# A gated attention unit with a channel mixer: z of batch 0 turned by TensorE, loads of v, z and u moved in GpSimd's queue

## The chip, the cores and the metric

The kernel runs on one core of one Trainium2 chip. The time is the device time of the core in microseconds. Before the change it is 1044.64 us, the median of 6 runs (1041.26 to 1045.92).

## The reference

There are 8 batches, each of 3136 rows; u and v have 256 columns, z has 64. Two functions follow each other:

```python
scores = (1 / S) * z @ z.T
attn = maximum(scores, 0) ** 2
x = u * (attn @ v)                       # first function
h = x.T @ U @ V                          # rank 32, mixes the rows
m = x + h.T
out = m + maximum(m @ w_ch1, 0) @ w_ch2  # 256 -> 1024 -> 256
```

## The kernel before, in words

**Tiles.** The 3136 rows make 25 tiles of 128, the last (number 24, NF in the code) of 64 rows. The scores are symmetric, so for each tile j only 13 of 25 blocks are computed (`score`, L256: two matmuls of 64 rows, ACT's relu at L273, DVE's square at L275) and kept in `A[j]`. The other 12 blocks of an output tile are transposes of stored ones: `turn` (L293) has SP's queue turn `A[o]` into a `strip` by a transposing DMA, four outputs ahead of use.

**z.** A score needs z with its 64 columns on the partitions. `load_z` (L160) has GpSimd's queue load z, cast to bf16; `double_z` (L171) has DVE write each tile twice side by side; `turn_z` (L181) has SP's queue turn the result into `zT` by transposing DMAs; `extend_z` (L188) has DVE copy the first 12 tiles behind the last, so that blocks can wrap around. In batch 0 this is the start of everything.

**Outputs.** The loop at L739 takes a batch's 25 output tiles, i = 0 to 24, starting from tile 12 (o = (12 + i) mod 25). Outputs go in pairs that share two PSUM banks: i = 0 and 1, 2 and 3, up to 10 and 11, then tile 24 alone (i = 12), then 13 and 14 and so on. `attend_steps` (L381) gives an output's 25 steps of matmuls A x v (L333, half of the rows each; L367 for tile 24); between them `_spread` puts the score steps of other tiles, those of the next batch among them. `close_pair` (L342) adds the two banks (ACT L347, DVE L348) and multiplies by u (DVE L357) into `x_bf`. `load_u` (L313) has GpSimd's queue load the u of the pair after the one that opens; there are two u buffers, so it waits for L357 of the pair before.

**The mixer.** While batch b attends, the mixer of batch b - 1 runs beside it: `rank` (L416) at i = 0, `low_rank` (L463, its DVE step at L484) for seven chunks of tiles at i = 2, 3, 6, 7, 10, 11, 14, each followed by `turn_x` (L439), a transposing DMA of `x_bf` into `ut` on SP's queue. After outputs 4, 8, 13 and 17 come two bursts each (`bursts_of`, L557): the up matmuls of a chunk (L499, relu on ACT at L506) merged with the down matmuls of the chunk before (L530), each finished pair stored by GpSimd's queue (L549) once DVE has made `o_sb` (L541). The last batch's mixer stands alone at the end.

**What orders the work.** [...] All plain loads and stores stand in GpSimd's queue (POOL), all transposing DMAs in SP's. A POOL instruction that waits holds everything behind it: an out store waits for DVE's L541, a u load for L357. For the next batch, `load_z` stands at i = 1, `double_z` at 5, `turn_z` at 7 and 10, `extend_z` at 11, and the nine parts of v at i = 1, 3, 4, 5, 7, 8, 10, 11, 12 (in batch 0: z loaded in `start_up`, the rest at 9, 11, 13 and 14, and v parts at 8, 9, 10, 12, 14 to 18). Two buffers hold v, by the parity of the batch.

**The opening.** `start_up` (L575) loads z of batch 0 in three parts, then v tiles 8 to 11, doubles and turns z, and holds GpSimd's other v loads back by a copy that reads `zT` (L584). Then scores and matmuls of the first eight outputs run together, and weights and z of batch 1 are loaded.

Of the kernel before, what the change touches and what calls it, by code (L numbers as in the profile page):

```python
# [42 lines left out]
def kernel(  # L43
# [61 lines left out]
    def pair_psum():  # L105
        return ps2_pool.tile([P, 2, 512], FP32, name="ps2")
# [9 lines left out]
    zT = persist.tile([P, NT + HALF, P], BF16, name="zT")  # L116
    zT_flat = zT.rearrange("p t c -> p (t c)")
    v_both = [persist.tile([P, NT, D], BF16, name=f"v{k}") for k in range(2)]
    x_bf = persist.tile([P, XR // 4, 4 * D], BF16, name="x_bf")
    A = [persist.tile([P, NB * P], BF16, name=f"A{j}") for j in range(NT)]  # L120

# [33 lines left out]
        return ap.rearrange("p (t a c) -> p t a c", a=ND, c=P)  # L155


    z_tiles = {}

    def load_z(b, parts):  # L160
        z_c = stage.tile([P, NT, dqk], BF16, name="z_c")
        for t0, t1 in parts:
            pool_dma(out=z_c[:, t0:t1, :], in_=rows(z[b])[:, t0:t1, :])
        for r in halves:
            pool_dma(out=z_c[r, NF, :], in_=z[b, NF * P :, :])
        z_tiles[b] = z_c

    def upto(t1):
        return t1 if t1 < NF else NT

    def double_z(b, parts):  # L171
        z_c = z_tiles[b]
        z_bf = stage.tile([P, NT, 2, dqk], BF16, name="z_bf")
        z_tiles[b] = z_bf
        for t0, t1 in parts:
            for h in range(2):
                nc.vector.tensor_copy(
                    out=z_bf[:, t0 : upto(t1), h, :], in_=z_c[:, t0 : upto(t1), :]
                )

    def turn_z(b, parts):  # L181
        z_bf = z_tiles[b]
        for t0, t1 in parts:
            transpose(
                out=zT[:, t0 : upto(t1), :],
                in_=z_bf[:, t0 : upto(t1), :, :].rearrange("p t h c -> p (t h c)"),
            )
    def extend_z():  # L188
        nc.vector.tensor_copy(out=zT[:, NT:, :], in_=zT[:, :HALF, :])
# [185 lines left out]
    def after(b, o):  # L375

        t0, n = pair_of(o)
        i = place(t0) + n
        return (b, turns(i)) if i < NT else (b + 1, turns(0))

    def attend_steps(b, o):  # L381
        t0, n = pair_of(o)
        last = t0 + n - 1
        js = [(o - k) % NT if k < NB else (o + k - HALF) % NT for k in range(NT)]
        js.remove(NF)

        def step(i):
            if i == 0 and o == t0:
                open_pair(b, o)
                if after(b, o)[0] < B:  # L390
                    load_u(*after(b, o))
            if o == NF:
                if i < NT - 1 and i % 2:
                    for n in (i - 1, i):
                        for h in range(2):
                            quarter(b, js[n], n, h)
                elif i == NT - 1:
                    quarter(b, NF, i, 0)
# [12 lines left out]
        return [lambda i=i: step(i) for i in range(NT)]  # L411


# [161 lines left out]
    def start_up():  # L575
        parts = ((8, 16), (0, 8), (16, NF))
        load_z(0, parts)
        v_parts = [(8, 12), (12, 18), (3, 8), (0, 3), (18, NF), (NF, NT)]
        load_v(0, v_parts[0])
        double_z(0, parts)  # L580
        turn_z(0, parts)
        extend_z()
        mark = small.tile([P, D], BF16, name="mark", tag="t1_sb")
        nc.gpsimd.tensor_copy(out=mark[:1, :1], in_=zT[:1, 7, :1])  # L584
        for part in v_parts[1:]:
            load_v(0, part)
        nc.gpsimd.memset(U_bf[:, NF, :], 0.0)
        outs = [FIRST + i for i in range(NG)]
        c0 = FIRST * P
# [15 lines left out]
        def make(pair):  # L605
            if all(LEAD - 1 - HALF <= j < FIRST for j in pair):
                todo = []
                for j in pair:
                    at = (FIRST - j) * P
                    where[j] = A[j][:, at : at + NG * P]  # L610
                    todo.append((j, c0, NG * P, where[j]))
                score(todo)
            else:
                room = rooms.pop(0)
                for i, j in enumerate(pair):
                    where[j] = room[:, i, :]
                score([(j, c0, NG * P, room) for j in pair])
# [9 lines left out]
                seen.append(j)  # L627

        for i, pair in enumerate(pairs):
            make(pair)  # L630
            if i > 5 and i % 2:
                nxt.pop(0)()
            if i > 1:
                use(pairs[i - 2])
# [82 lines left out]
    def run(steps):  # L717
        for s in steps:
            s()
# [5 lines left out]
    for b in range(B):  # L725
        more = b + 1 < B
        begin = 0 if b else 2 * NG
        bursts = bursts_of(b - 1) if b else []
        burst_at = {4: (0, 1), 8: (2, 3), 13: (4, 5), 17: (6, 7)}
        z_load, z_double, z_half, z_turn = (1, 5, 7, 10) if b else (None, 9, 11, 13)  # L730
        soon = next_at if b else next_first
        v_at = (1, 3, 4, 5, 7, 8, 10, 11, 12) if b else (8, 9, 10, 12, 14, 15, 16, 17, 18)
        v_at = dict(zip(v_at, V_PARTS))
        ahead = dict(zip((2, 3, 6, 7, 10, 11, 14), range(NC)))
        first = []
        if b == 0:
            for j, k1 in [(NT - 1, NB)] + [(j, NB if j < 3 else FIRST - j) for j in range(FIRST)]:
                first += score_steps(j, 0, k1)
        for i in range(begin, NT):  # L739
            o = turns(i)  # L740
            fill = []
            if b == 0:
                if i < z_turn:
                    n = _ceil_div(len(first), z_turn - i)
                    fill, first = first[:n], first[n:]
            else:
                fill = [s for key in own_at[i] for s in score_steps(*key)]
            if more:
                fill += [s for key in soon[i] for s in score_steps(*key)]
                if i == z_load:  # L750
                    load_z(b + 1, WHOLE)
                if i == z_double:
                    double_z(b + 1, WHOLE)
                if i == z_half:
                    turn_z(b + 1, ((FIRST, NF),))
                if i == z_turn:
                    turn_z(b + 1, ((0, FIRST),))
                if i == z_turn + 1:
                    extend_z()
                if i in v_at:  # L760
                    load_v(b + 1, v_at[i])
            main = attend_steps(b, o)
            if b and i in ahead:
                main.insert(14 if (i + (i > FIRST)) % 2 == 0 else 8, lambda c=ahead[i]: low_rank(b - 1, c))
            _spread(main, fill)
            if i + AHEAD < NT:
                turn(b, turns(i + AHEAD))
            elif more:
                turn(b + 1, turns(i + AHEAD - NT))
            elif i == NT - AHEAD:  # L770
                turn_x(b, 0)
            if b == 0 and i in weights:
# [57 lines left out]
```

## Time and profile before

| what | us |
|---|---|
| median of 6 runs | 1044.64 |
| the profiled execution, its own time | 1045.92 |
| its span in the profile | 1043.9 |
| TensorE busy with matmuls | 993.4 |
| ACT busy | 616.6 |
| DVE busy | 529.3 |
| GpSimd waiting at u loads (L317) for DVE's L357 | 421.5 |
| GpSimd waiting at out stores (L549) for DVE's L541 | 297.8 |
| first matmul after the start of the span | 10.32 |

"Busy" is the union of an engine's instructions; matmuls overlap, so a busy TensorE isn't one at its peak. The mean granted clock of TensorE was 0.993 of full speed. The DMA engines were busy nearly throughout (mean 162 GB/s): transposing DMAs on SP's queue took 60.6% of their time and plain loads and stores on GpSimd's queue 28.0%. A waits line says which instruction waited for which, how long in total, how often and the longest. In a timeline, a row is a start and a length in microseconds, then engine, line, operation and tiles, how many instructions were merged, and in brackets the idle time of the engine before it and what ended it.

### The profile page before, as it was taken

To read this page: it belongs to the slowest core of one execution; us is meant where nothing else is said; L and a number is where in the kernel's file an instruction comes from. 1 tells how busy PE (TensorE), PEld (TensorE's weight loads), DVE (VectorE), ACT (ScalarE), POOL (GpSimd) and SP (SyncE) were. 2 spreads that over 40 slices of the span, in tenths; PEclk is the share of its full clock that TensorE was granted. 3 is DMA by queue.
4 is the path that set the end of the run, shared out by engine and by line. 5 is a ranking of instruction groups with operands and counts; after the bars stand their busy time and mean duration, and the time that the engine had idled before them with its cause. 6 is when DMAs were issued, how large, how long until landed. Compare 5 with 4: busy or idle time off the path is not lost.

```text
span 1043.9 us, 31077 instructions
## 1 busy us (share of the span) xinstructions
PE 993.4 (95%) x13791; PEld 789.2 (76%) x13831; DVE 529.3 (51%) x946; ACT 616.6 (59%) x830; POOL 172.0 (16%) x319
## 2 busy tenths in 40 slices
PE   5877999999999999999999999999999999999998
PEld 4666878788677877778777887878867788787856
DVE  4766654456544555445554465545654356542242
ACT  5965674566646666366764577646675566743154
POOL 4121212112121111211212111121211110011000
PEclk9998999999999999999999999999999999999999
DMA  9999989889797997977989789997989888678532
GB/s 164 189 174 177 175 151 188 164 168 170 148 193 164 168 180 146 181 162 165 181 156 186 150 159 167 179 172 161 167 150 181 167 171 148 127 141 158 129 90 98
DMA packets 417990, 168.71 MB, mean 162 GB/s; under 512 B 392768, under 2 KB 402704, under 8 KB 417856
## 3 DMA queue, kind: packets, MB, share of 16 engines
q1 hardware_dynamic: 388272, 99.98, 60.6%
q0 software_dynamic: 29584, 66.75, 28.0%
q8 instruction: 108, 1.77, 0.7%
q14 instruction: 26, 0.21, 0.1%
HBM read 61.88 MB, written 25.69 MB: 84 GB/s over the span
## 4 chain that ended last, share of the span: by engine, by line
PE 82%; DMA 9%; ACT 4%; DVE 3%; issue 1%; POOL 0%; SPq 0%; ACTq 0%; DVEq 0%; POOLq 0%
PE ps L333 42%; PE ps L530 17%; PE ps L499 15%; PE ps L260 6%; DMA ut<-x_bf 4%; DMA zT<-z_bf 3%; ACT A L273 2%; DMA strip<-A 2%; ACT relu L506 1%; PE ps L424 1%; PE ps L470 1%; DVE x_bf L484 1%; PE ps L367 1%; DVE A L275 1%; DVE both L348 1%
## 5 line engine op out<-in xcount | busy, mean ns | idle before, releaser
L273 ACT ACTIVATE A<-ps 128x832 bf16<-128x832 f32 (+8 forms) x469 | 351.3, 763 | 179.3 <-PE ps L260 162.2
L333 PE MATMUL ps<-v,A 64*128 64x256 bf16 x4864 | 336.3, 271 | 3.2 <-DVE both L348 2.0
L275 DVE TENSOR_TENSOR A<-A 128x832 bf16<-128x832 bf16 (+8 forms) x469 | 239.6, 524 | 143.6 <-ACT A L273 140.8
L333 PE MATMUL ps<-v,strip 64*128 64x256 bf16 x4420 | 308.4, 270 | 0.0
L506 ACT ACTIVATE relu<-ps 128x1024 bf16<-128x1024 f32 (+2 forms) x224 | 202.4, 916 | 142.2 <-PE ps L499 142.2
L333 PEld LDWEIGHTS <-A 64*128 64x128 bf16 x4864 | 243.4, 95 | 44.1 <-issue 12.0
L333 PEld LDWEIGHTS <-strip 64*128 64x128 bf16 x4420 | 225.1, 94 | 30.2
L499 PE MATMUL ps<-ut,w_bf 128*128 128x512 bf16 (+2 forms) x856 | 200.1, 352 | 14.1 <-DMA ut<-x_bf 5.9
L541 DVE TENSOR_TENSOR o_sb<-ps,x_bf 128x512 f32<-128x512 f32 (+1 forms) x104 | 69.7, 670 | 278.7 <-PE ps L530 276.2
L530 PE MATMUL ps<-w_bf,relu 128*128 128x256 bf16 x1600 | 204.8, 273 | 0.0
L530 PEld LDWEIGHTS <-relu 128*128 128x128 bf16 x1600 | 155.9, 98 | 46.4 <-issue 1.3
L260 PE MATMUL ps<-zT 64*128 64x416 bf16 (+10 forms) x933 | 155.6, 319 | 23.4 <-DMA zT<-z_bf 21.2
L499 PEld LDWEIGHTS <-w_bf 128*128 128x128 bf16 x896 | 84.8, 98 | 76.5 <-issue 14.2
L317 POOL DMA_DIRECT2D u_sb<-in_u_dram x96 | 53.4, 557 | 459.1 <-DVE x_bf L357 421.5
L347 ACT COPY both<-ps 128x512 f32<-128x512 f32 (+1 forms) x104 | 58.9, 567 | 83.9 <-PE ps L333 73.3
L549 POOL DMA_DIRECT2D out_dram<-o_sb x84 | 45.9, 546 | 297.8 <-DVE o_sb L541 297.8
L348 DVE TENSOR_TENSOR both<-ps,both 128x512 f32<-128x512 f32 (+1 forms) x104 | 69.3, 666 | 30.1 <-ACT both L347 29.7
L260 PEld LDWEIGHTS <-zT 64*128 64x128 bf16 x933 | 52.3, 95 | 32.6 <-DMA zT<-z_bf 21.5
L357 DVE TENSOR_TENSOR x_bf<-both,u_sb 128x512 bf16<-128x512 f32 (+1 forms) x104 | 69.8, 672 | 3.6
L484 DVE TENSOR_TENSOR x_bf<-ps,x_bf 128x512 bf16<-128x512 f32 (+1 forms) x112 | 65.4, 626 | 8.6 <-PE ps L470 8.6
L195 POOL DMA_DIRECT2D v<-in_v_dram x61 | 34.2, 568 | 0.0
L470 PE MATMUL ps<-t_sb,V_bf 64*128 64x256 bf16 x200 | 24.0, 271 | 2.3 <-DVE x_bf L484 0.5
(42 smaller groups left out, 173.7 us busy)
## 6 DMA issues: line engine op xcount, KB each, us to landing
u_sb<-in_u_dram POOLq DMA_DIRECT2D x96, 256.0 KB, 4.1
out_dram<-o_sb POOLq DMA_DIRECT2D x84, 256.0 KB, 2.5
v<-in_v_dram POOLq DMA_DIRECT2D x57, 192.0 KB, 5.3
strip<-A SPq DMA_TRANSPOSE x196, 5.3
out_dram<-o_sb SPq DMA_DIRECT2D x12, 256.0 KB, 2.0
z_c<-in_z_dram POOLq DMA_DIRECT2D x7, 384.0 KB, 6.1
w_bf<-in_moe_w_ch_dram POOLq DMA_DIRECT2D x2, 512.0 KB, 7.9
u_sb<-in_u_dram POOLq DMA_DIRECT2D x16, 64.0 KB, 3.4
```

Source lines behind the costliest of these rows:

```text
L260: mm(out=ps[:, k, :n], lhsT=zT[halves[k], j, :], rhs=zT_flat[halves[k], c : c + n], start=True, stop=True,)
L273: nc.scalar.activation(out=dst, in_=src, func=AF.Relu, scale=sc)
L275: nc.vector.tensor_tensor(out=dst, in0=dst, in1=dst, op=ALU.mult)
L333: mm(out=acc[t0][h][:, (o - t0) * D : (o - t0 + 1) * D], lhsT=w[halves[h]], rhs=v_both[b % 2][halves[h], j, :], start=start, stop=stop, **kw,)
L347: nc.scalar.copy(out=both[:, :w], in_=banks[1][:, :w])
L348: nc.vector.tensor_tensor(out=both[:, :w], in0=banks[0][:, :w], in1=both[:, :w], op=ALU.add)
L357: nc.vector.tensor_tensor(out=x_at(b, t0, n), in0=split(both[:, :w]), in1=u_sb[:, :n, :].rearrange("p t (a c) -> p t a c", c=P), op=ALU.mult,)
L484: nc.vector.tensor_tensor(out=q, in0=split(ps[h][:, : len(ks) * D]), in1=q, op=ALU.add)
L499: mm(out=ps[:, i, :w], lhsT=w1_bf[:, db, (hp + i) * P : (hp + i + 1) * P], rhs=uT[c][:, db, len(chunks[c]) * P - w :], start=(db == 0), st ...
L506: nc.scalar.activation(out=relus[c][:, hp : hp + 2, :w], in_=ps[:, :, :w], func=AF.Relu)
L530: mm(out=ps[:, k * D : (k + 1) * D], lhsT=relus[c][:, ht, q : q + P], rhs=w2_bf[:, ht, :], start=(ht == 0), stop=(ht == NH - 1),)
L541: nc.vector.tensor_tensor(out=o_sb[:p, :nk, :].rearrange("p t (a c) -> p t a c", c=P), in0=split(ps[:p, : nk * D]), in1=x_at(b, t, nk)[:p] ...
```

## The change

Four edits in one:

- z of batch 0: after `load_z`, GpSimd makes an identity matrix (`memset`, `affine_select`) and issues all six v loads at once; each part of z is doubled and turned by matmuls against the identity into PSUM, from where ACT and DVE copy it to `zT`. The third part is turned between the second and the third pair of scores. The transposing DMAs of the opening and the holding copy go.
- The next batch's v and z, from batch 1 on: v part n is issued in the middle of burst n (parts 7 and 8 in burst 7), z in two parts in bursts 0 and 1; `double_z` stands at i = 6 instead of 5.
- `load_u` stands at step 16 of a pair's first output instead of step 0.
- v of batch 1 is loaded at i = 9, 11, 12, 14, 16, 18, 20, 22, 23.

```diff
     def load_z(b, parts):
-        z_c = stage.tile([P, NT, dqk], BF16, name="z_c")
+        if b not in z_raw:
+            z_raw[b] = stage.tile([P, NT, dqk], BF16, name="z_c")
+        z_c = z_raw[b]
         for t0, t1 in parts:
             pool_dma(out=z_c[:, t0:t1, :], in_=rows(z[b])[:, t0:t1, :])
-        for r in halves:
-            pool_dma(out=z_c[r, NF, :], in_=z[b, NF * P :, :])
-        z_tiles[b] = z_c
+            if t1 == NF:
+                for r in halves:
+                    pool_dma(out=z_c[r, NF, :], in_=z[b, NF * P :, :])
...
+    def turn_on_pe(b, parts):
+
+        z_bf = z_tiles[b]
+        for t0, t1 in parts:
+            ps = pair_psum().rearrange("p i (t c) -> p i t c", c=P)
+            for t in range(t0, t1):
+                k, n = divmod(t - t0, 4)
+                mm(
+                    out=ps[:, k, n, :],
+                    lhsT=z_bf[:, t, :, :].rearrange("p h c -> p (h c)"),
+                    rhs=eye,
+                    start=True,
+                    stop=True,
+                )
+            for k, copy in enumerate((nc.scalar.copy, nc.vector.tensor_copy)):
+                ta, tb = t0 + 4 * k, min(t0 + 4 * k + 4, t1)
+                if ta < tb:
+                    copy(out=zT[:, ta:tb, :], in_=ps[:, k, : tb - ta, :])
...
             if i == 0 and o == t0:
                 open_pair(b, o)
-                if after(b, o)[0] < B:
-                    load_u(*after(b, o))
+            if i == 16 and o == t0 and after(b, o)[0] < B:
+                load_u(*after(b, o))
...
         parts = ((8, 16), (0, 8), (16, NF))
         load_z(0, parts)
-        v_parts = [(8, 12), (12, 18), (3, 8), (0, 3), (18, NF), (NF, NT)]
-        load_v(0, v_parts[0])
-        double_z(0, parts)
-        turn_z(0, parts)
-        extend_z()
-        mark = small.tile([P, D], BF16, name="mark", tag="t1_sb")
-        nc.gpsimd.tensor_copy(out=mark[:1, :1], in_=zT[:1, 7, :1])
-        for part in v_parts[1:]:
+        nc.gpsimd.memset(eye, 1.0)
+        nc.gpsimd.affine_select(
+            out=eye,
+            in_=eye,
+            pattern=[[1, P]],
+            base=0,
+            channel_multiplier=-1,
+            compare_op=ALU.is_equal,
+            fill=0.0,
+        )
+        for part in [(8, 12), (12, 18), (3, 8), (0, 3), (18, NF), (NF, NT)]:
             load_v(0, part)
+        for part in parts[:2]:
+            double_z(0, [part])
+            turn_on_pe(0, [part])
+        double_z(0, parts[2:])
...
         for i, pair in enumerate(pairs):
+            if i == 2:
+                turn_on_pe(0, ((16, NF), (NF, NT)))
+                extend_z()
             make(pair)
...
-        z_load, z_double, z_half, z_turn = (1, 5, 7, 10) if b else (None, 9, 11, 13)
+        z_double, z_half, z_turn = (6, 7, 10) if b else (9, 11, 13)
         soon = next_at if b else next_first
-        v_at = (1, 3, 4, 5, 7, 8, 10, 11, 12) if b else (8, 9, 10, 12, 14, 15, 16, 17, 18)
-        v_at = dict(zip(v_at, V_PARTS))
+        v_at = dict(zip((9, 11, 12, 14, 16, 18, 20, 22, 23), V_PARTS)) if b == 0 else {}
...
-                if i == z_load:
-                    load_z(b + 1, WHOLE)
...
-                run(_merge(up, down))
+                steps = _merge(up, down)
+                if more:
+                    loads = [lambda k=k: load_v(b + 1, V_PARTS[k]) for k in ((n,) if n < NC else (n, n + 1))]
+                    if n < 2:
+                        loads.append(lambda n=n: load_z(b + 1, (((0, FIRST), (FIRST, NF))[n],)))
+                    steps = _merge(steps, loads)
+                run(steps)
```

More of the change, by code (lines that the diff above doesn't have):

```diff
@@ L118 @@
     v_both = [persist.tile([P, NT, D], BF16, name=f"v{k}") for k in range(2)]
+    eye = persist.tile([P, P], BF16, name="eye")
     x_bf = persist.tile([P, XR // 4, 4 * D], BF16, name="x_bf")
@@ L155, in split @@
         return ap.rearrange("p (t a c) -> p t a c", a=ND, c=P)
-    z_tiles = {}
+    z_raw, z_tiles = {}, {}
     def load_z(b, parts):
-        z_c = stage.tile([P, NT, dqk], BF16, name="z_c")
+        if b not in z_raw:
+            z_raw[b] = stage.tile([P, NT, dqk], BF16, name="z_c")
+        z_c = z_raw[b]
         for t0, t1 in parts:
             pool_dma(out=z_c[:, t0:t1, :], in_=rows(z[b])[:, t0:t1, :])
-        for r in halves:
-            pool_dma(out=z_c[r, NF, :], in_=z[b, NF * P :, :])
-        z_tiles[b] = z_c
+            if t1 == NF:
+                for r in halves:
+                    pool_dma(out=z_c[r, NF, :], in_=z[b, NF * P :, :])
     def upto(t1):
@@ L171, in double_z @@
     def double_z(b, parts):
-        z_c = z_tiles[b]
-        z_bf = stage.tile([P, NT, 2, dqk], BF16, name="z_bf")
-        z_tiles[b] = z_bf
+        if b not in z_tiles:
+            z_tiles[b] = stage.tile([P, NT, 2, dqk], BF16, name="z_bf")
+        z_c, z_bf = z_raw[b], z_tiles[b]
         for t0, t1 in parts:
```

## The prediction

> **What bounds the kernel now.** I read the page first, then the waits by engine, the timeline of the opening and of the longest gap, and the chain that ended last, for the length of a batch.
>
> ```profile
> PE 993.4 (95%) x13791; PEld 789.2 (76%) x13831; DVE 529.3 (51%) x946; ACT 616.6 (59%) x830; POOL 172.0 (16%) x319
> ```
>
> TensorE is the bound: busy 993.4 of 1043.9 us. All that a rearrangement of loads can win is the other 50 us: 10.3 before the first matmul, 10.9 in one gap of batch 0, the rest small gaps. The waits view says which transfers end them.
>
> ```profile
> DVE zT L189 <- DMA zT<-z_bf: 26.3, 8, 14.1
> PE ps L260 <- DMA zT<-z_bf: 21.2, 2, 10.9
> ACT A L273 <- DMA strip<-A: 11.1, 5, 4.2
> PE ps L499 <- DMA ut<-x_bf: 5.9, 8, 1.2
> ```
>
> Columns: total us, times, longest. All four are transposing DMAs of SP's queue. The two waits of L260 are the opening and the long gap, here from the timeline:
>
> ```profile
> 1.24 1.75 POOL L163 DMA_DIRECT2D z_c<-in_z_dram  x3 [0.79 <-POOLq L816]
> 4.23 1.26 DVE L177 COPY z_bf<-z_c 128x512 bf16<-128x512 bf16 x4 [4.23 <-DMA z_c<-in_z_dram]
> 4.92 5.65 SPq L184 DMA_TRANSPOSE zT<-z_bf  x3
> 10.32 1.03 PE L260 MATMUL ps<-zT 64*128 64x512 bf16 x4 [10.32 <-DMA zT<-z_bf]
> 10.96 2.07 ACT L273 ACTIVATE A<-ps 128x512 bf16<-128x512 f32 x4 [8.95 <-PE ps L260]
> 12.48 1.94 PE L333 MATMUL ps<-v,A 64*128 64x256 bf16 x16
> ...
> 74.06 4.55 SPq L184 DMA_TRANSPOSE zT<-z_bf  x1
> 84.56 0.23 PE L260 MATMUL ps<-zT 64*128 64x64 bf16 x2 [10.91 <-DMA zT<-z_bf]
> ```
>
> z is there at 4.23, turned at 10.3. And from the chain, the matmuls that open each mixer, one per batch (start, us):
>
> ```profile
> 120.32 1.53 PE ps L424 x50
> 244.87 1.53 PE ps L424 x50
> 371.13 1.53 PE ps L424 x50
> 497.67 1.53 PE ps L424 x50
> 624.11 1.53 PE ps L424 x50
> 747.57 1.53 PE ps L424 x50
> 874.31 1.53 PE ps L424 x50
> ```
>
> The batches last 124.6, 126.3, 126.5, 126.4, 123.5 and 126.7 us. The same code once ran in 123.5, with no gap beyond one of 0.31 us; the six together are 13.3 us above six times that. In the PE rows the excess looks like this (batch 3):
>
> ```profile
> 387.01 1.90 PE L499 MATMUL ps<-ut,w_bf 128*128 128x512 bf16 x7 [0.93 <-DMA ut<-x_bf]
> ...
> 441.87 1.02 PE L499 MATMUL ps<-ut,w_bf 128*128 128x512 bf16 x4 [1.75 <-ACT A L273]
> ```
>
> The second is a PSUM buffer whose reader, ACT, may not overwrite an A that a strip transpose is still reading.
>
> **What a load costs a transpose.** From the page's DMA table: queue q0 took 28.0% of 16 x 1043.9 us for 29584 packets, 0.158 us each; q1 60.6% for 388272, 0.026 us. A v part of three tiles is 128 packets, 8 per DMA engine: 1.3 us. A strip is 12 x 128 rows, 96 packets per engine: 2.5 us. So each v part in flight can put a transpose 1.3 us later, a u pair or half of z about as much.
>
> **Part 1: z of batch 0 on TensorE.** Removed: three transposes, 4.92 to 10.27 for the part that the first score needs. Added: 25 matmuls against an identity, six PSUM copies, and on GpSimd a memset and an affine_select that make the identity. [...]
>
> [...] For the upper side no row is near (GpSimd's memsets are 0.1 to 0.2 us)[...]. By the rows the identity would be there at 4.0 + 0.2 + 0.3 = 4.5 (a memset of 32 columns takes 0.21; the select is put a little above it)[...]. I take 10.5[...].
>
> From identity time T, in program order:
> - 8 matmuls at 0.11 us (the first 16 L333, from 12.48, take 1.94, so 0.12): T+0.95.
> - ACT copy of 512 columns 0.60 (L273 form with 512 columns: 604 ns), then DVE copy 0.69 (it waits for ACT): T+2.3.
> - DVE doubling of the second z part, 2 x 0.33 (L177 form 128x512: 330 ns). It stands behind that DVE copy, so it no longer runs while the identity is awaited: T+2.95.
> - 8 matmuls: T+3.85. Then the first score; its ACT reader starts after ACT's copy of the second part, T+4.5. Before, this row was at 10.96.
> - The third part's nine matmuls and three copies stand between score pairs: 0.6 + 0.3 us more on ACT, which from there on sets the pace (9.82 us busy in the ten from 20 to 30, from the table of windows).
>
> With T = 10.5: 15.0 - 10.96 + 0.9 = +4.9; DVE's copies among the squarings and one more hand-over between PSUM buffers, +0.6: **+5.5 us**. With T = 4.5: **-0.5**. With T = 14.5: +9.5. The v loads start at 10.5 instead of 11.36 and do not decide. What hid the turning before, SP's queue, was idle, so nothing is won there.
>
> **Part 2: v of batch 1 by pairs.** Before the second half of zT goes out in batch 0 (the long gap), the outputs up to it asked for v parts 0 to 5 in the old order, 0 to 3 in the new. In the trace POOL had run ahead: of those six, one had landed by 55.4, when SP's queue began to run without a break until zT landed at 84.51 (issues of 2.3 to 5.1 us each, where a free queue takes 1.3). In that stretch the new order has four parts, the old five: one part, 1.3 us, and 0.2 for the lighter start. **-1.5 us**, between 0 and -4 (-4 if both late parts count fully). The granted clock, 0.50 from 80 to 85 us and 0.73 from 85 to 90 (table of windows), stays low after either gap.
>
> **Part 3: v and z of the next batch in the bursts.** The mixer bursts (11.4, 13, 13 and 7 us in a batch) issue no strip and wait for no transpose but ut. Before, z and four v parts were asked for at outputs 1 to 5 of a batch, where the strips and ut of chunks 0 and 1 are due, and three v parts at 10 to 12, where zT, ut and a strip are due: those are the gaps above. After, they follow POOL's out stores, which wait for DVE inside the burst. That holds from the second pair of bursts on. In the first pair v part 0, half of z and v part 1 stand ahead of the first store, behind the u load of output 4: POOL reaches them when the pair before closes (386 in batch 3), about where the burst starts (387.0). ut of chunk 1 is then on its way: its x_bf is ready at 382.6, and its issue at 386.35 was late only because SP was held 4.70 us by the strip ahead. Without z and three v parts at 371 to 386 I expect it near 383.5, landed by 389, for a burst that starts at 391.3. The doubling of z (2 x 0.98 us on DVE) moves from output 5 to 6 and turning stays at 7: no cost, cover is the 4 us of an output; without it, 0.5 us a batch. 84 stores share a burst with a v part: a store lands after 2.3 to 4.9 us, its buffer is next wanted after 6. No cost.
>
> Of the 13.3 us above the gap-free batch I take three quarters: **-10 us**, between -4 and -13.
>
> **Part 4: u at step 16.** 2 us later in an output, with a whole pair (over 7 us) before it is read, landing 4.1. POOL no longer stands at u waiting for the close with v loads queued behind (421.5 us of such waits). Its own price is nothing; it is what makes part 3 possible.
>
> **Sum.** +5.5 - 1.5 - 10 = -6.0 us. The profiled execution took 1045.92 (span 1043.9 and 2.0 around it): 1039.9. It lies 1.28 above the median 1044.64, so 1038.6 beside the median.
>
> **The rivals.**
> - [...] -0.5 - 1.5 - 10 = -12: 1032.6. Chance 0.18.
> - No change: the gaps go only in part, since the strips' own traffic (60.6% of the DMA engines) makes them too; batch 5 without gaps under the same loads speaks for chance timing. +5.5 - 1.5 - 4.5 = -0.5: 1044.1. Chance 0.20.
> - Slower, by one mechanism: POOL is not tied to TensorE, so in each of six batches v part 0, half of z and v part 1 go out just as ut of chunk 1 does, and 1.3 + 1.4 + 1.3 = 4 us of packets lie ahead of it. It decides from the point where that ut is issued after about 385.5 in batch 3's times: then it lands 2 us or more after 391.3. +12: 1050.6. Against it: x_bf ready at 382.6. Chance 0.12.
>
> **How the numbers follow.** Forecast 1038.6, chance 0.50, by itself 1034 to 1042.5 (T from 8 to 12, batches -7 to -13). About 0.3%, 3.1 us, is what a measurement of this kernel tells from no change: faster is below 1041.5. From the forecast 0.47 and the first rival 0.18, and a little of the second: 0.67. Same: 0.20. Slower: 0.13. The range 1031 to 1046 leaves out most of the slower rival and the ends.
>
> **What would show it.** Right: [...] the first ACT reading of a score near 15, L424 rows 124 us apart in batches 1 to 6, no PE wait for ut or for a strip's A at the third burst, the long gap near 9.5. Wrong: identity there by 5 us (first rival), periods still near 126 (second), or a new PE wait for ut four microseconds into the first burst of a batch (third). [...]

## The result, and the profile after

| | before | after |
|---|---|---|
| median in the comparison (us) | 1043.6 (42 runs) | 1053.55 (21 runs) |
| the profiled execution, its own time | 1045.92 | 1053.24 |
| its span | 1043.9 | 1051.5 |
| mean granted clock of TensorE | 0.993 | 0.985 |
| first mixer matmul of batch 1 | 120.32 | 120.92 |
| batches 1 to 6, first mixer matmul to first mixer matmul | 754.0 | 761.3 |

The ratio is 1.0076, interval 1.0055 to 1.0098; it and every ratio below leave out runs over 1.5% above the fastest of their kernel (3 of the 21 after), so it is less than the quotient of the two medians. The change makes the kernel slower; the forecast was 1038.6 and its range ended at 1046. In the changed kernel the code stands 22 lines lower from `extend_z` on: L180 is the doubling of z, L198 the turning on TensorE, L282 the score, L295 its reader on ACT and L297 its square on DVE, L355 the attention, L379 the product with u, L446 `rank`, L492 and L506 `low_rank` on TensorE and on DVE, L521 and L552 the mixer, L563 the sum ahead of a store.

First the rows of the waits view that answer to three of the four of before (the wait for ut has no row left), and one that is new:

```profile
DVE zT L211 <- DMA zT<-z_bf: 15.4, 3, 13.9
PE ps L282 <- DMA zT<-z_bf: 10.7, 1, 10.7
ACT A L295 <- DMA strip<-A: 0.9, 1, 0.9
PE ps L492 <- DVE x_bf L506: 13.0, 14, 3.6
```

What part 3 was to remove is gone: ACT waits 0.9 us for strips in place of 11.1, and TensorE no longer waits for ut at all. In its place stands a wait that was 0.5 us before: `low_rank` on TensorE, 13.0 us, for its own DVE step. The opening and the long gap, from the timeline (start, length; in brackets the idle time ahead and what ended it):

```profile
4.37 0.31 POOL L601 TENSOR_SCALAR_AFFINE_SELECT eye<-eye 128x128 bf16<-128x128 bf16 x1
...
4.88 1.04 PE L198 MATMUL ps<-eye,z_bf 128*128 128x128 bf16 x8 [4.88 <-DVE z_bf L180]
...
7.73 1.03 PE L198 MATMUL ps<-eye,z_bf 128*128 128x128 bf16 x8 [1.81 <-DVE z_bf L180]
...
9.34 1.09 ACT L295 ACTIVATE A<-ps 128x512 bf16<-128x512 f32 x2
...
13.14 1.93 PE L355 MATMUL ps<-v,A 64*128 64x256 bf16 x16
```

The matmul that ends the long gap of batch 0, from TensorE's timeline:

```profile
85.06 0.23 PE L282 MATMUL ps<-zT 64*128 64x64 bf16 x2 [10.72 <-DMA zT<-z_bf]
```

The identity is ready at 4.68, the end of its select's 0.31 us; the forecast had put it at 10.5. The first score is read 1.6 us sooner than before (9.34 against 10.96), but the first matmul of the attention comes 0.66 us later (13.14 against 12.48): the third part's nine matmuls and its copies stand in between. The long gap has its old length. So nearly all of the 7.6 us between the two spans lies in the batches (761.3 - 754.0 = 7.3). Their starts, from the chain that ended last:

```profile
120.92 1.53 PE ps L446 x50
...
246.28 1.53 PE ps L446 x50
...
376.20 1.53 PE ps L446 x50
...
503.12 1.53 PE ps L446 x50
...
628.36 1.53 PE ps L446 x50
...
755.27 1.53 PE ps L446 x50
...
882.18 1.53 PE ps L446 x50
```

The batches last 125.4, 129.9, 126.9, 125.2, 126.9 and 126.9 us. They are no longer irregular, as before; batches 3, 5 and 6 agree to 0.02 us, and so a regular cause is to be looked for. In batch 1 it looks like this, TensorE first, then DVE's queue:

```profile
156.45 0.27 PE L492 MATMUL ps<-t_sb,V_bf 64*128 64x256 bf16 x1 [1.40 <-DVE x_bf L506]
157.05 0.29 PE L492 MATMUL ps<-t_sb,V_bf 64*128 64x256 bf16 x2 [0.33 <-DVE x_bf L506]
```

```profile
152.38 0.69 DVE L379 TENSOR_TENSOR x_bf<-both,u_sb 128x512 bf16<-128x512 f32 x1
152.99 1.87 DVE L180 COPY z_bf<-z_c 128x1600 bf16<-128x1600 bf16 x2
154.78 1.02 DVE L297 TENSOR_TENSOR A<-A 128x768 bf16<-128x768 bf16 x2
155.71 1.28 DVE L506 TENSOR_TENSOR x_bf<-ps,x_bf 128x512 bf16<-128x512 f32 x2
```

and the same place in the kernel before, where the doubling (L177) stood an output earlier:

```profile
147.55 1.87 DVE L177 COPY z_bf<-z_c 128x1600 bf16<-128x1600 bf16 x2
...
152.10 0.69 DVE L357 TENSOR_TENSOR x_bf<-both,u_sb 128x512 bf16<-128x512 f32 x1
152.71 1.02 DVE L275 TENSOR_TENSOR A<-A 128x768 bf16<-128x768 bf16 x2
153.65 1.28 DVE L484 TENSOR_TENSOR x_bf<-ps,x_bf 128x512 bf16<-128x512 f32 x2
```

`low_rank` of chunk 2 (output 6) has filled a PSUM set (two banks) by 152.8. The two copies of the doubling now stand in DVE's queue ahead of the step that empties that set, which starts at 155.71 in place of 153.65: 2.06 us later, 1.8 when the 0.28 by which L379 too is later are taken off. `low_rank` of chunk 3 (output 7) is given the same PSUM set, so TensorE stands, 1.40 and 0.33 us. The same pair of gaps is in batches 1, 3, 4, 5 and 6. In batch 2, z had not even landed when DVE came to the doubling:

```profile
280.61 1.88 DVE L180 COPY z_bf<-z_c 128x1600 bf16<-128x1600 bf16 x2 [2.12 <-DMA z_c<-in_z_dram]
...
284.08 0.37 PE L492 MATMUL ps<-t_sb,V_bf 64*128 64x256 bf16 x1 [3.61 <-DVE x_bf L506]
```

A gap of 1.73 us doesn't yet explain 126.9. The table of windows does, laid over the time from each such gap on (batches 1 to 6; window, its length, busy time and instructions of TensorE, its weight loads, DVE, ACT and GpSimd, then the granted clock, the DMA share and GB/s):

```profile
156.45:159.86 3.41, 3.08 (x53) 2.85 (x54) 2.86 (x7) 1.61 (x3) 0.00 (x0) 1.00 0.50 93
282.90:289.73 6.83, 5.42 (x50) 4.22 (x51) 4.23 (x11) 1.73 (x3) 0.00 (x0) 0.50 0.61 113
412.70:416.11 3.41, 3.41 (x36) 2.84 (x34) 1.66 (x4) 1.07 (x2) 0.00 (x0) 0.51 0.80 148
538.70:542.11 3.41, 3.07 (x53) 2.84 (x54) 2.87 (x7) 1.61 (x3) 0.00 (x0) 1.00 0.50 91
665.20:668.61 3.41, 3.41 (x38) 2.92 (x35) 1.61 (x4) 1.57 (x3) 0.00 (x0) 0.51 0.92 169
791.50:794.91 3.41, 3.41 (x34) 2.90 (x35) 1.93 (x5) 0.76 (x1) 0.00 (x0) 0.50 0.71 131
```

Where the clock stays at 1.00 (batches 1 and 4) the batch lasts 125.4 and 125.2; where half the clock is granted for 3.41 us (3, 5, 6), 126.9. So a gap costs 1.8 us over the gap-free 123.5, and a window of half clock 1.6 more, about half its length. Batch 2 has a gap twice as long and a window twice as long.

Why batches 1 and 4 are spared can be read from where the windows lie. In the trace's record of the granted clock the low stretches of batches 2, 3, 5 and 6 begin at 282.95, 412.65, 665.24 and 791.53, which is 38, 74 and 37 steps of 3.413 us apart: in this trace the clock changes on one grid. Laid on that grid, batch 1 and then batch 3 read:

```profile
153.24:156.65 3.41, 2.01 (x35) 1.67 (x32) 3.41 (x6) 1.03 (x2) 0.55 (x1) 1.00 0.26 77
156.65:160.07 3.42, 3.09 (x57) 2.97 (x57) 2.79 (x8) 1.73 (x4) 0.00 (x0) 1.00 0.56 105
409.24:412.65 3.41, 1.68 (x29) 1.27 (x25) 3.41 (x8) 0.76 (x2) 0.03 (x1) 1.00 0.24 77
412.65:416.07 3.42, 3.42 (x38) 2.85 (x34) 1.71 (x4) 1.03 (x2) 0.00 (x0) 0.50 0.78 145
```

In batch 1 a border of the grid parts the two gaps, and TensorE is busy for 2.01 us of the step with the longer one; in batch 3 both gaps lie in one step, 1.68 us are left, and the next step gets half the clock (5 and 6 are like 3, and 4 like 1).

The sum of the profiled executions: the transfer waits of before gave back all of the 13.2 us above six gap-free batches; the gaps brought 12.5 (six times 1.73, and 2.1 more in batch 2), the windows about 8 (an estimate: half of 17.1, less what was idle in them); the opening and the gap of batch 0 together 0.6. That makes about +8, and 7.6 was measured.

### The profile page after: what moved, and what is told of

Same layout as the page of the kernel before. It is cut to its first block, busy times and chain, and to the rows that moved or that the text cites. A ratio compares the mean times of both kernels' runs of the same rounds, so it can differ in the third digit from the quotient of the medians.

```text
span 1051.5 us, 31147 instructions
## 1 busy us (share of the span) xinstructions
PE 1004.3 (96%) x13816; PEld 796.8 (76%) x13856; DVE 531.9 (51%) x949; ACT 619.2 (59%) x834; POOL 176.4 (17%) x326
## 4 chain that ended last, share of the span: by engine, by line
PE 88%; DVE 4%; ACT 4%; DMA 2%; issue 1%; SPq 0%; POOL 0%; DVEq 0%; ACTq 0%; POOLq 0%
PE ps L355 46%; PE ps L552 16%; PE ps L521 15%; PE ps L282 6%; ACT A L295 2%; ACT relu L528 1%; PE ps L492 1%; DVE z_bf L180 1%; PE ps L389 1%; PE ps L446 1%; DMA z_c<-in_z_dram 1%; DVE A L297 1%; DVE x_bf L506 1%; DMA zT<-z_bf 1%; DVE both L370 1%
## 5 line engine op out<-in xcount | busy, mean ns | idle before, releaser
L295 ACT ACTIVATE A<-ps 128x832 bf16<-128x832 f32 (+8 forms) x469 | 351.4, 763 | 182.2 <-PE ps L282 174.0
L355 PE MATMUL ps<-v,A 64*128 64x256 bf16 x4864 | 339.3, 273 | 3.2 <-DVE both L370 2.0
L297 DVE TENSOR_TENSOR A<-A 128x832 bf16<-128x832 bf16 (+8 forms) x469 | 239.4, 524 | 149.3 <-ACT A L295 147.1
L355 PE MATMUL ps<-v,strip 64*128 64x256 bf16 x4420 | 313.1, 273 | 0.0
L355 PEld LDWEIGHTS <-A 64*128 64x128 bf16 x4864 | 244.8, 95 | 45.0 <-issue 12.1
L355 PEld LDWEIGHTS <-strip 64*128 64x128 bf16 x4420 | 228.1, 95 | 31.5
L563 DVE TENSOR_TENSOR o_sb<-ps,x_bf 128x512 f32<-128x512 f32 (+1 forms) x104 | 69.7, 670 | 280.6 <-PE ps L552 269.6
L521 PE MATMUL ps<-ut,w_bf 128*128 128x512 bf16 (+2 forms) x856 | 200.1, 352 | 5.9 <-ACT relu L528 3.8
L552 PE MATMUL ps<-w_bf,relu 128*128 128x256 bf16 x1600 | 204.8, 273 | 0.0
L552 PEld LDWEIGHTS <-relu 128*128 128x128 bf16 x1600 | 155.9, 98 | 46.3 <-issue 1.3
L282 PE MATMUL ps<-zT 64*128 64x416 bf16 (+10 forms) x933 | 156.8, 321 | 13.5 <-DMA zT<-z_bf 10.7
L521 PEld LDWEIGHTS <-w_bf 128*128 128x128 bf16 x896 | 84.9, 98 | 67.3 <-issue 15.6
L379 DVE TENSOR_TENSOR x_bf<-both,u_sb 128x512 bf16<-128x512 f32 (+1 forms) x104 | 69.8, 672 | 3.7
L282 PEld LDWEIGHTS <-zT 64*128 64x128 bf16 x933 | 52.9, 96 | 23.3 <-DMA zT<-z_bf 11.0
L506 DVE TENSOR_TENSOR x_bf<-ps,x_bf 128x512 bf16<-128x512 f32 (+1 forms) x112 | 65.5, 626 | 9.6 <-PE ps L492 9.6
L492 PE MATMUL ps<-t_sb,V_bf 64*128 64x256 bf16 x200 | 24.3, 273 | 14.0 <-DVE x_bf L506 13.0
```

Source lines behind the costliest of these rows:

```text
L282: mm(out=ps[:, k, :n], lhsT=zT[halves[k], j, :], rhs=zT_flat[halves[k], c : c + n], start=True, stop=True,)
L295: nc.scalar.activation(out=dst, in_=src, func=AF.Relu, scale=sc)
L297: nc.vector.tensor_tensor(out=dst, in0=dst, in1=dst, op=ALU.mult)
L355: mm(out=acc[t0][h][:, (o - t0) * D : (o - t0 + 1) * D], lhsT=w[halves[h]], rhs=v_both[b % 2][halves[h], j, :], start=start, stop=stop, **kw,)
L379: nc.vector.tensor_tensor(out=x_at(b, t0, n), in0=split(both[:, :w]), in1=u_sb[:, :n, :].rearrange("p t (a c) -> p t a c", c=P), op=ALU.mult,)
L506: nc.vector.tensor_tensor(out=q, in0=split(ps[h][:, : len(ks) * D]), in1=q, op=ALU.add)
```

## The experiments

The theory after this reading: the place of the doubling is the whole loss, and the rest of the change is a gain of about 11 us. The rival: z of the next batch lands late because it is loaded in the burst (as in batch 2), and the gap would come with the doubling anywhere. Others: the opening on TensorE costs something that the opening doesn't show; u late or v in pairs does harm. Each ratio is to runs of the kernel before made beside it (medians 1041.66 to 1042.82).

### The doubling, put elsewhere

**Changed kernel, doubling at output 8.**

```diff
-        z_double, z_half, z_turn = (6, 7, 10) if b else (9, 11, 13)
+        z_double, z_half, z_turn = (8, 8, 10) if b else (9, 11, 13)
```

> The changed kernel with the doubling of z moved from output 6 to output 8 (and the first half of the turning from 7 to 8); all else as changed. Theory D (the two doubling copies of 0.94 us stand in DVE's queue ahead of low_rank's DVE step at output 6, TensorE waits 1.7 us for it in every batch and runs at half clock for a window after): the 1.4 and 0.33 us waits of L492 for L506 vanish, the half-clock windows of batches 1 to 6 too, the batches last about 123.3 us, the kernel about 1031 to 1034. Rival L (the loads inside the bursts are what makes the batches long): batches stay near 126, about 1050.

Measured: 1032.73, ratio 0.9907 (0.9877 to 0.9936). The six batches last 741.5 us in place of 761.3, and from 270 to 292 us, where batch 2 of the changed kernel has its low clock, the granted clock is 1.00. Its waits view has left of the wait at L492:

```profile
PE ps L492 <- DVE x_bf L506: 0.5, 2, 0.3
```

So the place of the doubling, output 6 in place of 8 (the first half of the turning, which needs it, moves from 7 to 8 with it), turns a gain of 0.9% into a loss of 0.8%.

**Kernel before, only the doubling at output 6.**

```diff
-        z_load, z_double, z_half, z_turn = (1, 5, 7, 10) if b else (None, 9, 11, 13)
+        z_load, z_double, z_half, z_turn = (1, 6, 7, 10) if b else (None, 9, 11, 13)
```

> The kernel before with nothing changed but the doubling of z at output 6 instead of 5. D: the same 1.7 us wait of low_rank's matmuls in each of six batches, 10 us, and half-clock windows worth 1.7 us each after most of them, so 1055 to 1060. L: no change, 1043.

Measured: 1052.17, ratio 1.0075 (1.0053 to 1.0096): the loss of the whole change, from this alone, with z loaded as early as ever, though less than the 1055 to 1060 expected. From its waits:

```profile
PE ps L470 <- DVE x_bf L484: 10.9, 14, 1.4
...
PE ps L499 <- DMA ut<-x_bf: 1.7, 4, 0.7
```

The longest is 1.4, as in five batches of the changed kernel, and the wait for ut has shrunk from 5.9 to 1.7 us. So the two losses lie partly on top of each other: while TensorE stands for DVE, transfers come in. That goes some way to explain why the doubling costs 9 us in the batches here (762.8 against 754.0) and 20 in the changed kernel (761.3 against 741.5); the wait for strips stays (12.0 us, 11.1 before). No part's price can be read from the sum alone.

**Changed kernel, z as before** (loaded whole at output 1, doubled at 5; v in the bursts stays).

```diff
-        z_double, z_half, z_turn = (6, 7, 10) if b else (9, 11, 13)
+        z_load, z_double, z_half, z_turn = (1, 5, 7, 10) if b else (9, 11, 13)
...
+                if i == z_load:
+                    load_z(b + 1, WHOLE)
...
-                    if n < 2:
-                        loads.append(lambda n=n: load_z(b + 1, (((0, FIRST), (FIRST, NF))[n],)))
```

> The changed kernel with z of the next batch loaded whole at output 1 and doubled at 5, as before; v stays in the bursts, u late, z of batch 0 on TensorE. D: no wait of L492, and most of the waits for ut gone; batches 123.5 to 124.5, 1033 to 1037. L: the v loads in the bursts still cost, about 1048.

Measured: 1031.95, ratio 0.9882 (0.9848 to 0.9917); the batches last 123.5 to 123.8. It can't be told from the doubling at 8: loading z in the bursts neither wins nor costs, once its doubling is out of the way.

**Changed kernel, doubling at output 6, but behind that output's steps.**

```diff
-                if i == z_double:
-                    double_z(b + 1, WHOLE)
...
             _spread(main, fill)
+            if more and i == z_double:
+                double_z(b + 1, WHOLE)
```

> The changed kernel, its doubling of z still at output 6 but put behind that output's attention and low_rank steps instead of ahead of them. If the place ahead of low_rank in VectorE's queue is the cause of the 1.73 us gaps, they go, and with them the half-clock windows behind them: about 1032, batches 123.5. If output 6 itself is the cause (z not landed, or the copies beside that output's squarings, whatever the order), the time stays within 0.5% of 1053.

Measured: 1040.2, ratio 0.9979 (0.9959 to 0.9998). Between the two expectations. The wait at L492 is gone, so the order in DVE's queue is its cause and not the output. But the copies now stand ahead of the next chunk's step, and the attention waits for that one; DVE, then TensorE:

```profile
151.10 1.87 DVE L180 COPY z_bf<-z_c 128x1600 bf16<-128x1600 bf16 x2
152.89 0.51 DVE L297 TENSOR_TENSOR A<-A 128x704 bf16<-128x704 bf16 x1
153.32 1.01 DVE L506 TENSOR_TENSOR x_bf<-ps,x_bf 128x512 bf16<-128x512 f32 x2
```

```profile
154.06 1.03 PE L355 MATMUL ps<-v,A 64*128 64x256 bf16 x10 [0.72 <-DVE x_bf L506]
```

That gap of 0.72 us stands in all six batches, and each lasts 124.6 or 124.7: none is longer by the 1.6 us of a window of half clock, and the mean clock of the span is 0.995 (0.985 in the changed kernel). So in this execution 0.72 us, six times, cost 6.4 us against the doubling at 8 (747.9 against 741.5) and brought no window of half clock that shows, where 1.73 us brought one in three batches of five. It is the shortest of the 22 (1035.73); the longer ones, with mean clocks down to 0.990, have no profile.

### Each other part by itself, on the kernel before

**Only v in the bursts** (z, u and the opening as before).

```diff
-        v_at = (1, 3, 4, 5, 7, 8, 10, 11, 12) if b else (8, 9, 10, 12, 14, 15, 16, 17, 18)
-        v_at = dict(zip(v_at, V_PARTS))
+        v_at = dict(zip((8, 9, 10, 12, 14, 15, 16, 17, 18), V_PARTS)) if b == 0 else {}
...
-                run(_merge(up, down))
+                steps = _merge(up, down)
+                if more:
+                    loads = [lambda k=k: load_v(b + 1, V_PARTS[k]) for k in ((n,) if n < NC else (n, n + 1))]
+                    steps = _merge(steps, loads)
+                run(steps)
```

> The kernel before with only the v loads of batches 2 to 7 moved into the bursts (z at output 1, doubling at 5, u at step 0, the opening as before). D: v alone wins most of the 13 us of transfer waits, about 1034 to 1038. L: slower than before, 1046 to 1050.

Measured: 1031.66, ratio 0.9897 (0.9865 to 0.993). The batches add up to 742.1; TensorE no longer waits for ut, and of the waits for strips there is left

```profile
ACT A L273 <- DMA strip<-A: 1.6, 3, 0.7
```

The whole gain of the change lies in this part, and it needs none of the others.

**Only v of batch 1 by pairs; only u late.**

```diff
-        v_at = (1, 3, 4, 5, 7, 8, 10, 11, 12) if b else (8, 9, 10, 12, 14, 15, 16, 17, 18)
+        v_at = (1, 3, 4, 5, 7, 8, 10, 11, 12) if b else (9, 11, 12, 14, 16, 18, 20, 22, 23)
```

> The kernel before with only the v loads of batch 1 at outputs 9, 11, 12, 14, 16, 18, 20, 22, 23. The prediction's step: one v part less ahead of the second half of zT, the long gap of batch 0 about 1.5 us shorter, 1042. Rival, from the changed kernel's trace (two v parts issued together at 64.1, just ahead of the transposes that the gap waits for; gap 10.7): the gap stays at 10 to 12 us where the old order varies from 6.4 to 10.9 between executions, 1043 to 1047.

```diff
-                if after(b, o)[0] < B:
-                    load_u(*after(b, o))
+            if i == 16 and o == t0 and after(b, o)[0] < B:
+                load_u(*after(b, o))
```

> The kernel before with only u issued at step 16 of a pair's first output. The prediction's step: nothing by itself, 1043 with 2 us either way; the waits of L499 for ut and of L484 behind zT stay, since z and v are still loaded beside them. Rival (u at the pair's opening is part of what delays ut and zT): a part of the 13 us goes, 1036 to 1040.

Measured: 1042.08, ratio 1.0004 (0.9978 to 1.0031), and 1041.24, ratio 0.9993 (0.9969 to 1.0016). Neither is worth anything that shows. The long gap of batch 0 was 6.2 us in the one profile and 7.2 in the other, against 10.9 in that of before. That is the spread between executions and no gain: a kernel told further down, whose order there is that of before, had 6.9.

**Only the opening on TensorE** (identity, turning, v loads of batch 0 at once, as in the change).

> The kernel before with only z of batch 0 turned by TensorE. [...] By the changed kernel's trace (select at 4.37, first use of A by L355 at 13.14 against 12.48): [...] 0.7 us more, 1044; the row of the select near 4.4 again.

Measured: 1052.32, ratio 1.0074 (1.0037 to 1.0111). The prediction's +5.5 would make about 1048: the size could pass for it, the place can't. In the profiled execution the select stands at 4.38 again and batch 1 starts at 117.83, within 0.8 us of the two kernels just named, but the six batches last 761.1 us, with longer waits of the old kind, for ut and for PSUM sets; the longest of these are 2.2 us (L389 for L506) and 2.1 (L521 for ACT). Four kernels were to find out what in an opening could do that.

- The identity made, but not used:

```diff
+    eye = persist.tile([P, P], BF16, name="eye")
     x_bf = persist.tile([P, XR // 4, 4 * D], BF16, name="x_bf")
...
+        nc.gpsimd.memset(eye, 1.0)
+        nc.gpsimd.affine_select(
+            out=eye,
...
+        )
         nc.gpsimd.memset(U_bf[:, NF, :], 0.0)
```

> The kernel before, with only the identity added: its tile in SBUF (256 bytes a partition ahead of x_bf), the memset and the affine_select behind the v loads of the opening; nothing uses it. It asks why the opening on TensorE alone, added to the kernel before, came out at a ratio of 1.0074 though its opening ended only 0.3 to 0.8 us later. If the making of the identity or its place in memory is the cause, this kernel shows it too: about 1050, batches near 127. If the cause is the changed opening itself (three transposes fewer on SP's queue, v loads earlier), it stays at 1042 within 0.3%.

Measured: 1041.04, ratio 0.9991 (0.997 to 1.0012). Neither the identity nor the place of its tile in memory.

- The opening on TensorE, plus three transposes on SP's queue as before:

```diff
         double_z(0, parts[2:])
+        for t0, t1 in parts:
+            transpose(
+                out=A[NT - 1].rearrange("p (t c) -> p t c", c=P)[:, : upto(t1) - t0, :],
+                in_=z_tiles[0][:, t0 : upto(t1), :, :].rearrange("p t h c -> p (t h c)"),
+            )
```

> The kernel before with z of batch 0 turned by TensorE, as in the earlier run at 1.0074, plus three transposes of the same doubled z on SP's queue into a part of A that is written anew later, so that SP's queue has as many transposes as the kernel before. If the 7.7 us came from the number of transposes on that queue [...], they go: about 1043. If they came from the opening's other parts, or from the later start of batch 1 against the loads, the ratio stays near 1.007.

Measured: 1049.51, ratio 1.0082 (1.0054 to 1.011); the batches of its profile last 762.6 us. Not the number of transposes.

- The kernel before, with all v loads of batch 0 at once, z by DMA:

```diff
-        load_v(0, v_parts[0])
+        for part in v_parts:
+            load_v(0, part)
...
-        mark = small.tile([P, D], BF16, name="mark", tag="t1_sb")
-        nc.gpsimd.tensor_copy(out=mark[:1, :1], in_=zT[:1, 7, :1])
-        for part in v_parts[1:]:
-            load_v(0, part)
```

> The kernel before with one edit: the v loads of batch 0 no longer held back until the first part of zT has landed, so GpSimd issues them from about 5 us, as it does with the opening on TensorE; z is turned by DMA as before. The copy that held them took a buffer of the t1_sb pair, so the two buffers also change places through the kernel. If the early loads or that change of places make the later batches of the TensorE opening longer, this one has batches of about 127 too, and about 1050, apart from an opening up to 3 us longer (its transposes now land behind the v parts). If not, batches 1 to 6 keep a sum near 755.

Measured: 1062.49, ratio 1.0194 (1.0151 to 1.0236). In the profiled execution the batches add up to 749.9 us, no more than before, which speaks against the early loads as the cause. It is the shortest of its six, though (1052.21; the others 1060.87 to 1065.75), and no profile shows where the others have their 9 us more, so this run doesn't settle it. What it does show is the opening. The three transposes and the first score are

```profile
4.93 18.00 SPq L184 DMA_TRANSPOSE zT<-z_bf  x3
...
21.90 1.03 PE L260 MATMUL ps<-zT 64*128 64x512 bf16 x4 [21.90 <-DMA zT<-z_bf]
```

where before they took 5.65 us and the score stood at 10.32. My "up to 3 us" was far too little: the score is 11.6 us later, with five more v parts and two u loads issued beside the transposes, and from 12.66 on z of batch 1 and weights. That is the clearest reading here of what plain loads cost a transposing DMA, and it is what the small copy in the kernel before guards against. With z turned on TensorE the opening bears the same early loads: in the changed kernel they are issued from 4.63 on and the first score is read at 9.34 (22.55 here).

- The opening on TensorE, with the v loads held back as before:

```diff
-        for part in [(8, 12), (12, 18), (3, 8), (0, 3), (18, NF), (NF, NT)]:
-            load_v(0, part)
+        v_parts = [(8, 12), (12, 18), (3, 8), (0, 3), (18, NF), (NF, NT)]
+        load_v(0, v_parts[0])
...
         double_z(0, parts[2:])
+        mark = small.tile([P, D], BF16, name="mark", tag="t1_sb")
+        nc.gpsimd.tensor_copy(out=mark[:1, :1], in_=zT[:1, 7, :1])
+        for part in v_parts[1:]:
+            load_v(0, part)
```

> The opening on TensorE added to the kernel before, with the v loads of batch 0 again held back by the small copy until zT is there, and that copy's buffer taken from the t1_sb pair as before. If the early loads or the buffer are the cause of the longer batches, they go: batches of 125.7 in the mean, about 1043. If the turning on TensorE and its copies are the cause, the batches stay near 127 and the time near 1051.

Measured: 1050.04, ratio 1.0071 (1.005 to 1.0093). So the loss is there without the early loads: what is left is the turning on TensorE with its copies and the order they bring, and by what path it acts stays open. The profiled execution (1047.01) is one of the shorter of its 22 and its batches add up to 755.5, so it doesn't show where the 8 us of the median lie. What can be said is where it was seen: only with the v loads of the later batches among the strips. With v in the bursts, the changed kernel with z as before has this opening and takes 1031.95, the kernel before with v in the bursts has the old opening and takes 1031.66 (four runs each, and they differ in u and in v of batch 1 too).

### A better version

**v in the bursts, and the first half of zT of batch 1 turned on TensorE** at output 13 of batch 0, in place of the transpose that ends the long gap; the opening of the kernel before (excerpt; v as above, and the identity made behind the first v loads).

```diff
-                    turn_z(b + 1, ((0, FIRST),))
+                    if b:
+                        turn_z(b + 1, ((0, FIRST),))
+                    else:
+                        turn_on_pe(b + 1, ((0, 8), (8, FIRST)))
```

> Only v in the bursts, as in e4, and besides the first half of zT of batch 1 turned by twelve matmuls and PSUM copies at output 13 instead of by SP's queue (identity made after the first v loads). If the long gap of batch 0 is the transposing queue's backlog alone, the gap of 6 to 11 us and the half-clock windows after it (7 to 14 us, so 3.4 to 7 us lost) go: about 1017 to 1021. If the gap is set by something else (the strips behind it), a wait for a strip takes its place: 1026 to 1031.

Measured: 1029.11, ratio 0.9883 (0.9836 to 0.9931). In the profiled execution (span 1023.7) the long gap is down to one of 0.99 us, batch 1 starts at 111.38 (116.99 with v in the bursts alone) and the batches add up to 741.7. So the gap was the transposing queue's; but that execution, 1025.56, is the shortest of four that reach to 1034.63, the median stayed above the 1017 to 1021 of the first expectation, and no trace shows where the longer ones lose. By the intervals it can't be told from v in the bursts alone; both beat the kernel before and the changed kernel.

**The same, with an opening on TensorE too**, its doublings all ahead of the copies of zT and its third part turned later (excerpt).

```diff
...
+        double_z(0, parts)
+        turn_on_pe(0, parts[:2])
...
         for i, pair in enumerate(pairs):
+            if i == 6:
+                turn_on_pe(0, ((16, NF), (NF, NT)))
+                extend_z()
```

> The kernel before with v of the next batch in the bursts, the first half of zT of batch 1 turned by TensorE (that was 1029.1), and now the opening on TensorE as well, in an order of its own: all three doublings ahead of the copies of zT, and the third part turned only ahead of the seventh score pair. First score near 8.2 in place of 10.0, first matmul with v near 11.3 in place of 12.1: 0.8 us shorter, about 1028. If the opening on TensorE costs 7 us by itself, as it seemed to beside the loads of the kernel before, 1036.

Measured: 1031.44, ratio 0.9899 (0.9868 to 0.9929). The first score stands at 8.30, as expected, 1.7 us before that of the kernel above, yet nothing is won: the profiled execution has a gap of 3.34 us at 86.55, for ACT, and one of 3.44 at 668.44, for DVE's sum ahead of a store. Whether these belong to this version or to that execution was not tried.

## Why the prediction was wrong

**The step that failed** is in part 3: "The doubling of z (2 x 0.98 us on DVE) moves from output 5 to 6 and turning stays at 7: no cost, cover is the 4 us of an output; without it, 0.5 us a batch." The duration was right (1.87 for both). What was not asked is what is queued behind it on DVE and who waits for that: output 6 is one of the outputs with a `low_rank`, output 5 isn't. That DVE step is all that empties the PSUM set that the next chunk's `low_rank`, at output 7, is given; so TensorE stands 1.73 us, not 0.5, in five of the six batches (3.9 in batch 2, where z also landed late), and half clock follows in four. The term put at nothing measured 20 us in the changed kernel; alone on the kernel before it makes +0.75%. Without it the change is worth 0.9907, about -10 us, between the forecast's -6 and the first rival's -12. The kernel's own list of outputs for `low_rank` (2, 3, 6, 7, 10, 11, 14) had it in plain sight.

**Part 3, the rest.** The mechanism was right (the 1.3 us that a v part was to cost a transpose was an estimate from the packets of the profile, and no run shows it by itself), and its price too low: -10 was taken, three quarters of 13.3 (the rows give 13.2); v in the bursts alone gives 754.0 - 742.1 = -11.9 in the batches and ratio 0.9897. The slower rival (ut of chunk 1 behind the loads of the first burst) didn't come true: there is no wait of TensorE for ut. The "no change" rival (the strips' own traffic makes the gaps) is refuted by the same run.

**Part 1.** +5.5 rests on an identity that is ready at 10.5 and not at the 4.5 that the rows gave; that was an assumption of the author's, which no trace or run shows. The select's row is 0.31 us long and ends at 4.68; the first attention matmul is 0.66 us late. The -0.5 for an identity at 4.5 (GpSimd's z issues end at 4.0, then a memset and the select) was nearer: the first score was read 1.6 us sooner (2.0 in its working), but the third part and the hand-overs then took 2.3 us in place of 0.9 + 0.6. Added alone to the kernel before, this part does cost about 8 us, outside the opening (in two profiles of three, in the batches), for a cause that the runs narrowed down but didn't find; beside v in the bursts it costs nothing that shows. That the prediction had +5.5 here is no credit to its reason.

**Part 2.** -1.5 was taken; the long gap is 10.72 in place of 10.91, and the part alone gives 1.0004. Its bounds held 0. As the gap is anything from 6.2 to 10.9 us long in the profiles of the kernels that turn this zT by DMA, a step of 1.5 could not have been told there.

**Part 4.** "Its own price is nothing" holds (0.9993). "It is what makes part 3 possible" doesn't: v in the bursts brings all of its gain with u where it was.

**The clock.** The prediction looked at the granted clock only behind the long gap. In the trace of the changed kernel the low stretches of the batches last 3.41 us (6.83 in batch 2) and lie on one grid, and in batches 3, 5 and 6 such a stretch followed a step of the grid with 1.73 us without a matmul. Counted as gaps alone, the five batches with this gap would have lost 5 x 1.73 = 8.7 us; by the rows it is 3 x 1.6 = 4.8 us more. What exactly is counted stays open: in the kernel before, two windows with 1.75 us without a matmul (from 439.26 and from 558.73) were followed by the full clock. That the place of a gap on the grid differs between executions is not shown, but the times fit it: the five shortest runs of the changed kernel (up to 1048.09) have a mean clock of 0.992 or 0.993, all the others 0.984 to 0.990.

## What to carry to other kernels

When an operation is moved on an engine that isn't the bound, its duration isn't its price (1.87 us of DVE in each of six batches cost 20 us here): look up which instruction comes next in that engine's queue at the new place, which buffer that one empties, and who fills it next. Parts of a change that remove waits and parts that add them hide each other (9 us or 20 for the same move here), so each should be built alone on both sides before any of them is judged. Loads that go out in stretches where no transpose is due were the one lasting gain, 1% (ratio 0.9897).

## What the hardware showed that was not expected

- Two gaps of TensorE of 1.73 us together were followed by 3.41 us at half clock in three batches of five: where both fell into one step of the grid of 3.413 us on which this trace's clock changes, and not where a border parted them. With six gaps of 0.72 us, in one execution, the batches last 124.6 or 124.7 us, and no such stretch shows in their lengths.
- Three transposes issued among five more v parts and two u loads took 18.00 us in place of 5.65.
- The GpSimd select that makes the identity took 0.31 us on its first use (4.37 to 4.68); the v loads behind it in GpSimd's queue go out from 4.63 on.
- Turning z of batch 0 on TensorE moved the first attention matmul by less than 1 us, yet made three kernels some 8 us longer in the median; in two of their profiles the six later batches were 7 and 9 us longer than in that of before. Where the v loads lie elsewhere it did not show. The cause is open.
